# Splitting one product of the first pass's down stage a second time, and putting its queue in source order

## The chip, the cores and the metric

The kernel runs on one core of one Trainium2 chip. The metric is device microseconds (us) of one execution. A core has a matrix engine (PE, whose weight loads are listed as PEld), a vector engine (DVE), an activation engine (ACT), a third elementwise engine (POOL, which also issues the output transfers of this stage) and SyncE (SP), a queue that here does nothing but issue transfers (DMAs). Each engine works through its own list of instructions in order and waits on semaphores for the others.

## What is computed

The reference is a linear attention block and a SwiGLU feed-forward block on the same normalised input, joined by a gate:

```python
B, S, D, F = 1, 2048, 1024, 3584          # all inputs bfloat16, _rng.normal * 0.05
def _B_ref(x, w_gate, w_up, w_down):
    g = _silu(x @ w_gate)
    u = x @ w_up
    return (g * u) @ w_down
x  = A_x
xn = _layernorm(x, axis=-1)
s  = _A_ref(xn, A_wqkv, A_wo)              # linear attention, 32 heads of 32
g  = _silu(_B_ref(xn, B_w_gate, B_w_up, B_w_down))
return x + s * g
```

The change touches only `(g * u) @ w_down`, the silu behind it and `x + s * g`, and these only for one half of the tokens.

## The kernel before

After the attention part the kernel makes two passes over the tokens, 1024 tokens each (`passes = [1, 0]`). A pass has a gate/up stage, which leaves `h = g * u` transposed in one buffer (`hT`), and a down stage. In the first pass the down stage is `emit_down`, in the last pass `emit_down_m`.

Every large product is a Winograd form of Strassen's scheme: a matrix product cut in 2 x 2 blocks is made with seven block products instead of eight, with sums of blocks ahead of and behind them. In `emit_down` the blocks of `h` are A11, A12 (first 512 tokens) and A21, A22 (other 512 tokens), each over 14 chunks of 128 of the contraction (`NFG = 14`), and the output has two halves of 512 columns. So one block product is 4 token blocks `t` of 128, times 14 steps `k`, each a 128x128 by 128x512 matmul. The seven products are 392 such matmuls:

- phase a (`step_a`): the products M1 (into PSUM bank `dx`), M6 (`dy`), M7 and M5 (the two halves of `dzw`). Token blocks are taken in pairs, `hf = 0` (t = 0, 1) and then `hf = 1` (t = 2, 3). The second of a pair runs `LEAD = 6` steps behind the first. `evac_a` makes the sums from PSUM; for `hf = 0` it keeps them in SBUF (`kept`) and frees the banks.
- phase b (`step_b`): M2 = A12 B21 (into `dx`), M4 and M3 (into `dzw`). It takes `hf = 1` first, on top of what phase a left in PSUM, and then `hf = 0` in fresh banks, to which `evac_b` adds what was kept.

The weights come in packs: seven "a" packs of 1 MB (phase a), seven "b" packs of 768 KB (phase b), then the 1 MB packs of the next pass (`pk_g`, `pk_u`: g0, u0, g1, ...). There are eight pack buffers (`NPK`), so a pack can be loaded when an older one is no longer read. `load_w_to(n)` issues the loads of packs up to number n on SP.

The last pass makes four of its seven down products, M2 among them, with the same scheme one level further down: seven sub-products of 256 columns each, over 7 pairs of chunks (`l2_M`, `l2_p`). The weight sums for this are made during the first pass: `l2_early(2, j, False)` makes the four sums of pack j on POOL (L1137), into the unused end of the b pack, and `l2_early(2, j, True)` stores them by three DMAs on SP (L1129 to L1131). In the kernel before they stand in the step loop of phase b, `hf = 1`, one pack every second step, and only the last pass uses them.

The output: `fin` (L1219) multiplies a silu tile by `s`, adds `x` (L1223, L1224, both on DVE), has POOL issue the 128 KB output transfer (L1225) and calls `io_load` for a later tile's `x` and `s` (two 128 KB loads on SP, L1214 and L1215). There are five `io` buffers, so an `io_load` waits until the output transfer of the tile five places back has landed. The order of tiles is the list `fq`. Where `hold[0]` is set, `io_load` only notes the load in `io_due`. `fin` calls put into `deferred` are emitted one by one in the next pass's gate/up loop, each behind one step's evacuation.

The next pass's first operations on DVE are L996, L997 and L1010, which read the PSUM banks of its first group (`yb`, `zw`). `emit_Ssum` (L713 to L716) makes the four input sums for the next pass on DVE. PE runs group g0 (`emit_a`, 16 matmuls), u0 (`emit_a`, 16), then `emit_b` of g0 (12), which adds into g0's `xb` and the two halves of `zw`.

The order on PE, DVE, ACT and POOL is the source order everywhere. On SP it is the source order in the attention part and in the last pass (`manual_schedule`); in the first pass a scheduler places SP's instructions.

Of the kernel before, what the change touches and what calls it, by code (L numbers as in the profile page):

```python
# [21 lines left out]
def kernel(  # L22
# [931 lines left out]
    with ExitStack() as p3:  # L954
# [237 lines left out]
        for p in passes:  # L1192
            if p == passes[-1]:
                fq += [(p, t + dt, cc) for dt, cc in ((0, 0), (TPB, 1), (TPB, 0), (0, 1)) for t in range(TPB)]
                continue
            fq += [(p, t + TPB, 1) for t in range(TPB)]
            for hf in (1, 0):
                for t in (2 * hf, 2 * hf + 1):
                    fq += [(p, t + TPB, 0), (p, t, 1), (p, t, 0)]
# [29 lines left out]
        def emit_down(p, h, base, last, more_S, next_S):  # L1229
# [13 lines left out]

            def alloc(t, phase):
                x_ = pps.tile([P, CW], FP32, name="dx", tag="s")
                y_ = pps.tile([P, CW], FP32, name="dy", tag="s") if phase == "a" else None
                zw = ppd.tile([P, 2, CW], FP32, name="dzw", tag="d")
                bk[t] = (x_, y_, zw)
# [3 lines left out]

            def step_a(t, k):
                if k == 0:
                    alloc(t, "a")
                x_, y_, zw = bk[t]
                S1, S2, S3 = [v[:, k % 2, (t % 2) * P:(t % 2 + 1) * P] for v in s_ring[(t // 2, k // 2)]]
                f, l = k == 0, k == NFG - 1
                mm(x_[:], h[:, 2 * k, t * P:(t + 1) * P], wa(k, 3), f, l)
                mm(y_[:], S2, wa(k, 1), f, l)  # L1260
                mm(zw[:, 0, :], S3, wa(k, 2), f, l)
                mm(zw[:, 1, :], S1, wa(k, 0), f, l)

            def prods_b(t, k, fresh):
                x_, y_, zw = bk[t]
                f, l = fresh and k == 0, k == NFG - 1
                t2 = slice(TB + t * P, TB + (t + 1) * P)
                return [lambda: mm(x_[:], h[:, 2 * k + 1, t * P:(t + 1) * P], wb(k, 0), f, l),
                        lambda: mm(zw[:, 0, :], h[:, 2 * k + 1, t2], wb(k, 2), f, l),
                        lambda: mm(zw[:, 1, :], h[:, 2 * k, t2].bitcast(F16), wb(k, 1), f, l)]  # L1270

            def step_b(t, k, fresh):
                if k == 0 and fresh:
                    alloc(t, "b")
                for f in prods_b(t, k, fresh):
                    f()

            fin_e = (nc.vector, nc.vector, nc.sync if last else nc.gpsimd)
            pend = []

            def evac_a(t, keep):
# [5 lines left out]
                else:  # L1287
                    s1 = k2([P, CW], FP32, "s1")[:]
# [3 lines left out]
                nc.vector.tensor_tensor(out=s2, in0=y_[:], in1=s1, op=ALU.add)  # L1292
                nc.vector.tensor_tensor(out=s3, in0=zw[:, 0, :], in1=s2, op=ALU.add)
                c22 = k2([P, CW], FP32, "c22")[:] if keep else s3
                if keep:
                    nc.vector.tensor_tensor(out=u4, in0=zw[:, 1, :], in1=s2, op=ALU.add)
                nc.vector.tensor_tensor(out=c22, in0=zw[:, 1, :], in1=s3, op=ALU.add)
                g_ = k2([P, CW], BF16, "g22")[:]
                nc.scalar.activation(out=g_, in_=c22, func=ACT.Silu, scale=rch)
                pend.append(lambda: fin(p, t + TPB, 1, g_, *fin_e))  # L1300
                kept[t] = (s1, st[:, 1:3, :]) if keep else s2

            def evac_b(t, fresh):
                x_, _, zw = bk[t]
                d = m4.tile([P, 2, CW], FP32, name="dd", tag="m4")
                g_ = k2([P, 2, CW], BF16, "g12")
                g11 = k2([P, CW], BF16, "g11")[:]
                if fresh:
                    s1, s34 = kept[t]
                    c11 = k2([P, CW], FP32, "c11")[:]  # L1310
                    nc.vector.tensor_tensor(out=d[:], in0=zw[:], in1=s34, op=ALU.add)
                    nc.vector.tensor_tensor(out=c11, in0=x_[:], in1=s1, op=ALU.add)
                    nc.scalar.activation(out=g_[:], in_=d[:], func=ACT.Silu, scale=rch)
                    nc.scalar.activation(out=g11, in_=c11, func=ACT.Silu, scale=rch)
                else:
                    s2 = kept[t]
                    nc.vector.tensor_tensor(out=d[:], in0=zw[:], in1=s2[:, None, :].to_broadcast([P, 2, CW]),
                                            op=ALU.add)
                    nc.scalar.activation(out=g11, in_=x_[:], func=ACT.Silu, scale=rch)
                    nc.scalar.activation(out=g_[:], in_=d[:], func=ACT.Silu, scale=rch)  # L1320
                return [lambda: fin(p, t + TPB, 0, g_[:, 0, :], *fin_e),
                        lambda: fin(p, t, 1, g_[:, 1, :], *fin_e),
                        lambda: fin(p, t, 0, g11, *fin_e)]

            def finish(t):
                ps = [ppd.tile([P, 2, CW], FP32, name="dz", tag="d")[:, 0, :]]
                ps += [pps.tile([P, CW], FP32, name="df%d" % i, tag="s")[:] for i in range(3)]
                s1, s34 = kept[t]
                t1, t2 = slice(t * P, (t + 1) * P), slice(TB + t * P, TB + (t + 1) * P)
                hs_ = [slice(0, 3 * CW // 4), slice(3 * CW // 4, CW)]  # L1330
                for i in range(2):
                    nc.scalar.copy(out=ps[2 + i][:, 0:hs_[i].stop - hs_[i].start], in_=s1[:, hs_[i]])
                for q, (r0, cc) in enumerate(((t + TPB, 0), (t, 1))):
                    for k in range(NFG):
                        lhs = h[:, 2 * k, t2].bitcast(F16) if q else h[:, 2 * k + 1, t2]
                        mm(ps[q], lhs, wb(k, 2 - q), k == 0, k == NFG - 1)
                    d = k2([P, CW], FP32, "d%d" % q)[:]
                    g_ = k2([P, CW], BF16, "g%d" % q)[:]
                    nc.vector.tensor_tensor(out=d, in0=ps[q], in1=s34[:, q, :], op=ALU.add)
                    nc.scalar.activation(out=g_, in_=d, func=ACT.Silu, scale=rch)  # L1340
                    if q == 0:
                        f0 = (r0, cc, g_)
                fin(p, *f0, *fin_e)
                fin(p, r0, cc, g_, *fin_e)
                g11 = k2([P, CW], BF16, "g11")[:]
                for i, cs in enumerate(hs_):
                    o_ = ps[2 + i][:, 0:cs.stop - cs.start]
                    for k in range(NFG):
                        mm(o_, h[:, 2 * k + 1, t1], wb(k, 0)[:, cs], False, k == NFG - 1)
                    nc.scalar.activation(out=g11[:, cs], in_=o_, func=ACT.Silu, scale=rch)  # L1350
                    fin(p, t, 0, g11, *fin_e, cols=cs)

            NS = NFG + LEAD
            for hf in range(2):
                t0, t1 = 2 * hf, 2 * hf + 1
                for st in range(NS):
                    if st == 4:
                        while pend:
                            pend.pop(0)()
# [7 lines left out]
                    if st < NFG:  # L1367
                        step_a(t0, st)
                        if st == NFG - 1:
                            evac_a(t0, hf == 0)  # L1370
                    if st >= LEAD:
                        step_a(t1, st - LEAD)
                        if hf == 1 and (st - LEAD) % 2 == 1:
                            load_w_to(base + NWA + (st - LEAD) // 2 + 2)
                evac_a(t1, hf == 0)
# [3 lines left out]
            if not last:  # L1379
                emit_rcl()  # L1380
                emit_Ssum(passes[passes.index(p) + 1])
            for hf in (1, 0):
                t0, t1 = 2 * hf, 2 * hf + 1
                fresh = hf == 0
                endz = last and fresh
                for st in range(NFG if endz else NS):
                    if st == 4:
                        while pend:
                            pend.pop(0)()
                    if hf == 1 and not last and st % 2 == 1 and 2 in L2:  # L1390
                        if st // 2 < NQ:
                            l2_early(2, st // 2, False)
                        if 0 <= st // 2 - 2 < NQ:
                            l2_early(2, st // 2 - 2, True)
                    if st < NFG:
                        step_b(t0, st, fresh)
                        if st == NFG - 1:
                            fins = evac_b(t0, fresh)
                    if st >= LEAD and not endz:
                        step_b(t1, st - LEAD, fresh)  # L1400
                        if fresh and (st - LEAD) % 2 == 1:
                            load_w_to(base + 2 * NWA + (st - LEAD) // 2 + 2)
                if endz:
                    for f in fins:
                        f()
                    finish(t1)
                    break
                fins2 = evac_b(t1, fresh)
                for f in fins:
# [413 lines left out]
```

## Time and profile before

| | us |
|---|---|
| median of 3 runs (753.15 to 754.32) | 753.2 |
| the profiled execution | 753.18 |
| its span (the profile's clock) | 751.4 |
| first matmul of the first down stage | 413.86 |
| first matmul of phase b | 462.2 |
| first matmul of the second pass | 498.46 |
| first matmul of the last down stage | 667.83 |

All places in time below are microseconds from the start of the span. The 1.8 us between the span and the execution's time lie around the span. The stage that the change touches runs from 413.86 to 498.46, 84.6 us, and its phase b takes 36.2 us. The profile's rows give PE, DVE, ACT and POOL busy times; a matmul's listed duration (379 ns for 512 columns) includes a modelled pipeline end and overlaps the next one's, so the pace of matmuls is read from start to start.

### The profile page before, as it was taken

The page shows a single profiled execution, that of the slowest core. Times are in us where ns is not written, and L with a number is a line of the kernel's source. Part 1 is how long each engine was busy: PE and PEld are TensorE (multiplying, and loading weights), DVE is VectorE, ACT ScalarE, POOL GpSimd, SP SyncE. Part 2 cuts the span into 40 slices and gives each one's busy share as a digit, 9 for nine tenths or more (in the row PEclk, how much of TensorE's full clock was granted, in tenths as well). Part 3 has the DMA queues.
Part 4 walks back from the last instruction along what each step waited for, and adds up shares of the span by engine and source line. Part 5 has one row for each costly group of instructions (what it writes and reads, how often), then busy time and mean ns, then how long its engine had stood idle before and what let it go on. Part 6 is the DMA issues. An engine that isn't in the chain of part 4 may idle for free.

```text
span 751.4 us, 11202 instructions
## 1 busy us (share of the span) xinstructions
PE 744.1 (99%) x3899; PEld 364.9 (49%) x3899; DVE 580.9 (77%) x1054; ACT 383.0 (51%) x549; POOL 395.2 (53%) x492
## 2 busy tenths in 40 slices
PE   8999999999999999999999999999999999999997
PEld 3544544454454444444444444444444444467664
DVE  6687787887697788888889894557777778688857
ACT  5677766889965666756558411132322232332023
POOL 2444799998540265858585021910767576940000
PEclk9999999999999999999999999999999999999999
DMA  9957799869688668888799418789989889478852
GB/s 316 302 145 147 217 335 304 307 146 261 218 203 281 222 225 295 291 310 291 283 304 404 157 42 296 227 261 373 327 302 321 315 285 363 161 224 315 275 187 98
DMA packets 132472, 194.20 MB, mean 258 GB/s; under 512 B 36432, under 2 KB 106192, under 8 KB 122688
## 3 DMA queue, kind: packets, MB, share of 16 engines
q1 hardware_dynamic: 124224, 159.21, 65.7%
q0 software_dynamic: 6752, 31.79, 11.0%
q10 hardware_dynamic: 1440, 2.49, 1.0%
q8 instruction: 30, 0.49, 0.3%
q14 instruction: 26, 0.21, 0.1%
HBM read 122.68 MB, written 63.44 MB: 248 GB/s over the span
## 4 chain that ended last, share of the span: by engine, by line
PE 96%; DVE 2%; ACT 1%; DMA 0%; issue 0%; ACTq 0%; DVEq 0%
PE zw L968 26%; PE kv_ps L556 15%; PE xb L968 13%; PE yb L968 7%; PE q_ps L183 6%; PE dzw L1251 6%; PE dm L1484 6%; PE dm L1448 5%; PE dx L1251 3%; PE fx L818 3%; PE s_ps L776 3%; PE dy L1251 2%; PE kvz L578 1%; PE nd L745 1%; DVE w_sb L311 0%; PE fx L776 0%
## 5 line engine op out<-in xcount | busy, mean ns | idle before, releaser
L968 PEld LDWEIGHTS <-w_sb 128*128 128x128 f16 (+1 forms) x1568 | 152.1, 98 | 182.9 <-DMA w_sb<-pk_u 0.5
L968 PE MATMUL xb<-xnT,w_sb 128*128 128x512 bf16 x448 | 115.0, 379 | 0.0
L556 PE MATMUL kv_ps<-wkv_sb,xnT 128*128 128x512 bf16 x512 | 113.7, 379 | 0.6 <-ACT xnT L545 0.4
L968 PE MATMUL zw<-xnT,w_sb 128*128 128x512 bf16 x448 | 105.8, 379 | 0.0
L968 PE MATMUL zw<-S,w_sb 128*128 128x512 f16 x448 | 105.8, 379 | 0.0
L323 POOL TENSOR_TENSOR w_sb<-w_sb 128x512 f16<-128x512 bf16 x42 | 50.2, 1196 | 95.7 <-DVE w_sb L311 51.3
L288 ACT ACTIVATE w_sb<-w_sb 128x2048 bf16<-128x2048 bf16 x42 | 79.9, 1902 | 4.4 <-DMA w_sb<-in_B_w_up_dram 4.4
L556 PEld LDWEIGHTS <-xnT 128*128 128x128 bf16 x512 | 48.3, 98 | 55.9 <-ACT xnT L545 0.8
L1149 POOL TENSOR_TENSOR w_sb<-w_sb 128x512 f16<-128x512 f16 (+3 forms) x48 | 52.7, 1118 | 29.1 <-DMA w_sb<-wd 28.2
L1044 ACT ACTIVATE sg<-cg 128x1024 bf16<-128x1024 f32 x28 | 29.6, 1057 | 57.4 <-DVE cg L1037 57.4
L183 PE MATMUL q_ps<-xnT,wq_sb 128*128 128x512 bf16 x256 | 58.4, 379 | 0.0
L968 PE MATMUL yb<-S,w_sb 128*128 128x512 f16 x224 | 57.4, 379 | 0.0
L1037 DVE SCALAR_TENSOR_TENSOR cg<-zw,rc_all,s 128x1024 f32<-128x1024 f32 x28 | 35.9, 1284 | 24.5 <-PE zw L968 12.5
L996 DVE SCALAR_TENSOR_TENSOR s<-yb,rc_all,s 128x512 f32<-128x512 f32 x42 | 31.4, 749 | 27.3 <-ACT s L995 27.3
L324 POOL TENSOR_TENSOR w_sb<-w_sb 128x512 f16<-128x512 bf16 x42 | 50.4, 1201 | 3.3
L326 POOL TENSOR_TENSOR w_sb<-w_sb 128x512 f16<-128x512 bf16 x42 | 50.3, 1197 | 0.0
L325 POOL TENSOR_TENSOR w_sb<-w_sb 128x512 f16<-128x512 bf16 x42 | 50.2, 1196 | 0.0
L1225 POOL DMA_DIRECT2D out_dram<-io x16 | 8.7, 544 | 74.5 <-DVE io L1224 74.2
L995 ACT ACTIVATE s<-xb,rcl 128x512 f32<-128x512 f32 x14 | 9.6, 687 | 65.4 <-PE xb L968 65.4
L1251 PE MATMUL dx<-w_sb,hT 128*128 128x512 bf16 x112 | 42.4, 379 | 0.0
L995 ACT ACTIVATE s<-xb,rc_all 128x512 f32<-128x512 f32 x42 | 28.3, 674 | 21.8 <-issue 12.8
L311 DVE TENSOR_SCALAR w_sb<-w_sb,cs_all 128x2048 bf16<-128x2048 bf16 x35 | 36.7, 1048 | 2.8
(221 smaller groups left out, 1334.6 us busy)
## 6 DMA issues: line engine op xcount, KB each, us to landing
w_sb<-pk_g SPq DMA_DIRECT2D x27, 1024.0 KB, 7.3
pk_g<-w_sb SPq DMA_DIRECT2D x14, 1024.0 KB, 5.1
w_sb<-pk_u SPq DMA_DIRECT2D x14, 1024.0 KB, 7.5
pk_u<-w_sb POOLq DMA_DIRECT2D x13, 1024.0 KB, 5.5
w_sb<-l SPq DMA_DIRECT2D x12, 896.0 KB, 4.7
l<-w_sb POOLq DMA_DIRECT2D x9, 896.0 KB, 8.0
w_sb<-in_B_w_gate_dram SPq DMA_DIRECT2D x14, 512.0 KB, 6.5
w_sb<-in_B_w_down_dram SPq DMA_DIRECT2D x28, 256.0 KB, 4.5
```

Source lines behind the costliest of these rows:

```text
L183: nc.tensor.matmul(q_ps[:], lhsT=wq_sb[:, dc, g * P:(g + 1) * P], rhs=xn_ap(dc, btok), start=(dc == 0), stop=(dc == DC - 1))
L288: nc.scalar.activation(out=junk, in_=raw_view(key, t), func=ACT.Square, accum_out=asum[:])
L323: nc.gpsimd.tensor_tensor(out=T1, in0=b12, in1=b11, op=ALU.subtract)
L324: nc.gpsimd.tensor_tensor(out=T2, in0=b22, in1=T1, op=ALU.subtract)
L325: nc.gpsimd.tensor_tensor(out=T3, in0=b22, in1=b12, op=ALU.subtract)
L326: nc.gpsimd.tensor_tensor(out=T4, in0=b21, in1=T2, op=ALU.subtract)
L556: mm = nc.tensor.matmul(kv_ps[:], lhsT=xn_ap(dc, tok), rhs=wkv_sb[:, dc, c * CW:(c + 1) * CW], start=(dc == 0), stop=(dc == DC - 1))
L968: mm = nc.tensor.matmul(out, lhsT=lhs(k), rhs=rhs(k), start=(first and k == 0), stop=(k == HK - 1), skip_group_check=True)
L995: nc.scalar.activation(out=s1[:], in_=x_[:], func=ACT.Copy, scale=rc)
L1149: nc.gpsimd.tensor_tensor(out=b(o_), in0=b(a_), in1=b(b_), op=ALU.subtract)
L1251: nc.tensor.matmul(out, lhsT=lhs, rhs=rhs, start=first, stop=lastk, skip_group_check=True)
L1484: nc.tensor.matmul(out, lhsT=lhs, rhs=w[:, j], start=i == 1 and j == 0, stop=j == NQ - 1, skip_group_check=True)
```

## The change

M2 of the first pass's down stage is now made at the second level, as in the last pass, for all four token blocks at once (`l2_M2`), between the other two products of `hf = 1` and those of `hf = 0`. `step_b` issues only M4 and M3. Of `hf = 0`, four steps of the first block (and two of the second) stand inside `l2_M2` as `fill`; the second block now runs `LB = 2` steps behind, not 6. The weight sums (POOL) stand right behind the issue of the next b pack's load in phase a; four packs' stores stand ahead of phase b, three behind the matmuls of `hf = 1`. The left operand's sums (`lhs12`, `lhs34`) are four new DVE operations of 128x1792. `emit_Ssum` moves behind `l2_M2`. SP is in source order within `emit_down`. The order of output tiles, `fq`, follows. From behind `l2_M2` to behind the last matmul, `io_load` only notes its loads (`hold[0] = -1`); they are issued behind the load of the eighth pack of the next pass. Then `flush(2)` emits two `fin` calls, and the last two are deferred.

```diff
-            for hf in (1, 0):
-                for t in (2 * hf, 2 * hf + 1):
-                    fq += [(p, t + TPB, 0), (p, t, 1), (p, t, 0)]
+            fq += [(p, t + dt, cc) for t in (2, 3) for dt, cc in ((TPB, 0), (0, 1))]
+            fq += [(p, t, 0) for t in (1, 0, 3, 2)]
+            fq += [(p, t + dt, cc) for t in (0, 1) for dt, cc in ((TPB, 0), (0, 1))]
...
+            sp_man = ExitStack()
+            sp_man.enter_context(tc.manual_schedule(engines={mybir.EngineType.SP}))
...
-                return [lambda: mm(x_[:], h[:, 2 * k + 1, t * P:(t + 1) * P], wb(k, 0), f, l),
-                        lambda: mm(zw[:, 0, :], h[:, 2 * k + 1, t2], wb(k, 2), f, l),
-                        lambda: mm(zw[:, 1, :], h[:, 2 * k, t2].bitcast(F16), wb(k, 1), f, l)]
+                mm(zw[:, 0, :], h[:, 2 * k + 1, t2], wb(k, 2), f, l)
+                mm(zw[:, 1, :], h[:, 2 * k, t2].bitcast(F16), wb(k, 1), f, l)
...
+            def lhs12():
+                tt(l2_buf(5, 1), a21, a22)
+                tt(l2_buf(6, 2), sb[5], a11, ALU.subtract)
+            def lhs34():
+                tt(l2_buf(7, 0), a11, a21, ALU.subtract)
+                sb[3] = a21.bitcast(F16)
+                tt(sb[3], a12, sb[6], ALU.subtract)
...
+            def l2_M2(fill):
+                lo, hi = slice(0, CH), slice(CH, CW)
+                bank = [[pps.tile([P, CW], FP32, name="dm", tag="s")[:] for _ in range(2)] for r in range(2)]
+                K = [[kept[2 * r + i][0] for i in range(2)] for r in range(2)]
+                for r in range(2):
+                    l2_p(1, r, bank[r])
+                for r in range(2):
+                    nc.scalar.copy(out=bank[r][1][:, hi], in_=bank[r][0][:, lo])
+                for r in range(2):
+                    l2_p(2, r, bank[r])
+                for r in range(2):
+                    l2_p(5, r, bank[r])
+                    l2_p(6, r, bank[r])
+                    nc.scalar.copy(out=bank[r][1][:, lo], in_=bank[r][1][:, hi])
+                flush()
+                for r in range(2):
+                    l2_p(7, r, bank[r])
+                cs = [m4.tile([P, 2, CW], FP32, name="dc", tag="m4") for r in range(2)]
+                for r in range(2):
+                    (xw, zy), c = bank[r], cs[r]
+                    tt(c[:, 1, hi], zy[:, lo], K[r][1][:, hi])
+                    tt(c[:, 0, hi], zy[:, hi], K[r][0][:, hi])
+                    tt(c[:, 0, lo], xw[:, lo], K[r][0][:, lo])
+                    tt(c[:, 1, hi], xw[:, hi], c[:, 1, hi])
+                fill()
+                for r in range(2):
+                    l2_p(4, r, bank[r])
+                for r in range(2):
+                    (xw, zy), c = bank[r], cs[r]
+                    tt(c[:, 1, lo], zy[:, lo], K[r][1][:, lo])
+                    fins.append((2 * r + 1, 0, silu(c[:, 1], "g11")))
+                    l2_p(3, r, bank[r])
+                    tt(c[:, 0, hi], xw[:, hi], c[:, 0, hi])
+                    fins.append((2 * r, 0, silu(c[:, 0], "g11")))
...
                         if hf == 1 and (st - LEAD) % 2 == 1:
                             load_w_to(base + NWA + (st - LEAD) // 2 + 2)
+                            l2_early(2, (st - LEAD) // 2, False)
...
             load_w_to(base + 2 * NWA + 1)
-            if not last:
-                emit_rcl()
-                emit_Ssum(passes[passes.index(p) + 1])
...
+            lhs34()
+            emit_rcl()
+            for j in range(NQ - 3):
+                l2_early(2, j, True)
+            for st in range(NS):
+                if st < NFG:
+                    step_b(TPB - 2, st, False)
+                    if st == NFG - 1:
+                        flush()
+                        evac_b(TPB - 2)
+                if st >= LEAD:
+                    step_b(TPB - 1, st - LEAD, False)
+            for j in range(NQ - 3, NQ):
+                l2_early(2, j, True)
+            evac_b(TPB - 1)
+            LB, FB = 2, 4
+            def b0(st):
+                if st < NFG:
+                    step_b(0, st, True)
+                if st >= LB:
+                    step_b(1, st - LB, True)
+                if st == NFG - 1:
+                    flush()
+                    evac_b(0)
+            def fill():
+                for st in range(FB):
+                    b0(st)
+            l2_M2(fill)
+            emit_Ssum(passes[passes.index(p) + 1])
+            hold[0] = -1
+            for st in range(FB, NFG + LB):
+                load_w_to(base + 2 * NWA + (st - LB) // 2 + 1)
+                b0(st)
+            load_w_to(base + 3 * NWA + 1)
+            evac_b(1)
+            hold[0] = False
+            while io_due:
+                io_due.popleft()
+                io_load()
+            flush(2)
+            while fins:
+                deferred.append(lambda f=fins.popleft(): fin(p, *f, nc.vector, nc.vector, nc.gpsimd))
+            sp_man.close()
```

`flush(n)` emits up to n of the pending `fin` calls (all without a number). `l2_p(i, r, bank)` issues seven matmuls of 256 columns: sub-product i for the token blocks of pair r.

More of the change, by code (lines that the diff above doesn't have):

```diff
@@ L1227, in fin, with emit_down @@
                 io_load()
-        def emit_down(p, h, base, last, more_S, next_S):
+        def emit_down(p, h, base, more_S, next_S):
             def wa(k, q):
@@ L1242, in emit_down, with tt @@
             kept = {}
[L1244 to L1248, printed above, removed]
+            sp_man = ExitStack()
+            sp_man.enter_context(tc.manual_schedule(engines={mybir.EngineType.SP}))
             def mm(out, lhs, rhs, first, lastk):
                 nc.tensor.matmul(out, lhsT=lhs, rhs=rhs, start=first, stop=lastk, skip_group_check=True)
+            def tt(out, a, b_, op=ALU.add):
+                nc.vector.tensor_tensor(out=out, in0=a, in1=b_, op=op)
             def step_a(t, k):
                 if k == 0:
-                    alloc(t, "a")
+                    bk[t] = [pps.tile([P, CW], FP32, name=nm, tag="s") for nm in ("dx", "dy")]
+                    bk[t].append(ppd.tile([P, 2, CW], FP32, name="dzw", tag="d"))
                 x_, y_, zw = bk[t]
@@ L1262, in step_a, with step_b, flush, silu @@
                 mm(zw[:, 1, :], S1, wa(k, 0), f, l)
-            def prods_b(t, k, fresh):
-                x_, y_, zw = bk[t]
+            def step_b(t, k, fresh):
+                if k == 0 and fresh:
+                    bk[t] = [ppd.tile([P, 2, CW], FP32, name="dzw", tag="d")]
+                zw = bk[t][-1]
                 f, l = fresh and k == 0, k == NFG - 1
                 t2 = slice(TB + t * P, TB + (t + 1) * P)
-                return [lambda: mm(x_[:], h[:, 2 * k + 1, t * P:(t + 1) * P], wb(k, 0), f, l),
-                        lambda: mm(zw[:, 0, :], h[:, 2 * k + 1, t2], wb(k, 2), f, l),
-                        lambda: mm(zw[:, 1, :], h[:, 2 * k, t2].bitcast(F16), wb(k, 1), f, l)]
[L1272 to L1279, printed above, removed]
+                mm(zw[:, 0, :], h[:, 2 * k + 1, t2], wb(k, 2), f, l)
+                mm(zw[:, 1, :], h[:, 2 * k, t2].bitcast(F16), wb(k, 1), f, l)
+            fins = deque()
+            def flush(n=99):
+                while fins and n:
+                    fin(p, *fins.popleft(), nc.vector, nc.vector, nc.gpsimd)
+                    n -= 1
+            def silu(c, nm):
+                g_ = k2([P, CW], BF16, nm)[:]
+                nc.scalar.activation(out=g_, in_=c, func=ACT.Silu, scale=rch)
+                return g_
             def evac_a(t, keep):
@@ L1287, in evac_a @@
                 else:
-                    s1 = k2([P, CW], FP32, "s1")[:]
+                    s1 = x_spare[t - TPB // 2][:, 3, :]
                     s3 = k2([P, CW], FP32, "s3")[:]
@@ L1291, in evac_a @@
                 nc.scalar.copy(out=s1, in_=x_[:])
-                nc.vector.tensor_tensor(out=s2, in0=y_[:], in1=s1, op=ALU.add)
-                nc.vector.tensor_tensor(out=s3, in0=zw[:, 0, :], in1=s2, op=ALU.add)
+                tt(s2, y_[:], s1)
+                tt(s3, zw[:, 0, :], s2)
                 c22 = k2([P, CW], FP32, "c22")[:] if keep else s3
                 if keep:
-                    nc.vector.tensor_tensor(out=u4, in0=zw[:, 1, :], in1=s2, op=ALU.add)
-                nc.vector.tensor_tensor(out=c22, in0=zw[:, 1, :], in1=s3, op=ALU.add)
@@ L1298, in evac_a @@
[L1298 to L1304, printed above, removed]
+                    tt(u4, zw[:, 1, :], s2)
+                tt(c22, zw[:, 1, :], s3)
+                fins.append((t + TPB, 1, silu(c22, "g22")))
+                kept[t] = (s1, st[:, 1:3, :] if keep else s2[:, None, :].to_broadcast([P, 2, CW]))
@@ L1305, in evac_b @@
+            def evac_b(t):
                 d = m4.tile([P, 2, CW], FP32, name="dd", tag="m4")
                 g_ = k2([P, 2, CW], BF16, "g12")
[L1307 to L1351, printed above, removed]
@@ new lines, in evac_b, with l2_buf @@
+                tt(d[:], bk[t][-1][:], kept[t][1])
+                nc.scalar.activation(out=g_[:], in_=d[:], func=ACT.Silu, scale=rch)
+                fins.extend([(t + TPB, 0, g_[:, 0, :]), (t, 1, g_[:, 1, :])])
+            A = quads(h, 1, 0)
+            aq = [A[:, k].rearrange("p j (r t n) -> p j r t n", r=2, t=2) for k in range(2)]
+            a11, a12, a21, a22 = aq[0][:, :, :, 0], aq[1][:, :, :, 0], aq[0][:, :, :, 1], aq[1][:, :, :, 1]
+            sb = {}
+            def l2_buf(i, s):
+                t = sp.tile([P, HK, TB], F16, name="S%d" % s, tag="S%d" % s)
+                sb[i] = t[:].rearrange("p a b -> p (a b)")[:, 0:2 * NQ * P].rearrange("p (j r n) -> p j r n", j=NQ, r=2)
+                return sb[i]
@@ new lines, in lhs12, with l2_p @@
+            def lhs12():
[5 more added lines that the diff above has]
+                tt(sb[3], a12, sb[6], ALU.subtract)
+            def l2_p(i, r, bank):
+                half, y0 = {1: (0, 0), 2: (0, 0), 5: (0, 1), 3: (0, 1), 6: (1, 1), 7: (1, 0), 4: (1, 0)}[i]
+                out = bank[half][:, y0 * CH:(y0 + 1) * CH]
+                lhs = {1: a11, 2: a12, 4: a22}.get(i)
+                lhs = sb[i] if lhs is None else lhs
+                for j in range(NQ):
+                    w = w_tiles[(p, "b", j)][:].rearrange("p h a b -> p (h a b)")
+                    if i <= 3:
+                        k, c = {1: (0, 0), 2: (1, 0), 3: (1, 1)}[i]
+                        w = w[:, 0:6 * CW].rearrange("p (k q c n) -> p q k c n", k=2, q=3, c=2)[:, M_PACK[2][1], k, c]
+                    else:
+                        w = w[:, 6 * CW:8 * CW].rearrange("p (b n) -> p b n", b=4)[:, (5, 6, 7, 4).index(i)].bitcast(F16)
+                    mm(out, lhs[:, j, r], w, i == 1 and j == 0, j == NQ - 1)
@@ L1357, in emit_down @@
                     if st == 4:
-                        while pend:
-                            pend.pop(0)()
+                        flush()
                     if hf == 0:
@@ L1370, in emit_down @@
                             evac_a(t0, hf == 0)
+                            if hf == 1:
+                                lhs12()
                     if st >= LEAD:
@@ L1378, in emit_down @@
             load_w_to(base + 2 * NWA + 1)
-            if not last:
-                emit_rcl()
-                emit_Ssum(passes[passes.index(p) + 1])
[L1382 to L1409, printed above, removed]
-                    f()
-                if fresh:
-                    deferred.extend(fins2)
-                else:
-                    for f in fins2:
-                        f()
@@ new lines, in emit_down @@
+            evac_b(TPB - 1)
[6 more added lines that the diff above has]
+                if st == NFG - 1:
+                    flush()
+                    evac_b(0)
[5 more added lines that the diff above has]
+            hold[0] = -1
@@ L1788 @@
             else:
-                emit_down(p, h, base, last_pass, more_S, next_S)
+                emit_down(p, h, base, more_S, next_S)
             base += 2 * NWA
```

## The prediction

> **What bounds the kernel now.** I read the busy times and the chain of waits first, then the stretches around the stage.
>
> ```profile
> PE 744.1 (99%) x3899; PEld 364.9 (49%) x3899; DVE 580.9 (77%) x1054; ACT 383.0 (51%) x549; POOL 395.2 (53%) x492
> ...
> PE 96%; DVE 2%; ACT 1%; DMA 0%; issue 0%; ACTq 0%; DVEq 0%
> ```
>
> PE is the bound. In the table of stretches (busy us of PE, PEld, DVE, ACT, POOL, then granted clock, DMA share, GB/s) it has no gap in phase b, nor in the start of the second pass, where the DMA engines are almost full:
>
> ```profile
> 462.20:480.00 17.80, 17.80 (x84) 8.13 (x83) 9.63 (x13) 2.70 (x4) 8.96 (x15) 1.00 0.98 346
> 480.00:498.40 18.40, 18.40 (x87) 8.29 (x86) 9.63 (x15) 3.60 (x4) 8.90 (x14) 1.00 0.62 193
> 498.40:520.00 21.60, 21.60 (x102) 9.59 (x100) 18.55 (x28) 7.88 (x11) 2.70 (x5) 1.00 0.95 365
> ```
>
> So work taken off PE is gained whole, and a wait of PE is lost whole. The timeline of PE gives its paces (start, us, line, count):
>
> ```profile
> 1.49 4.07 PE L592 MATMUL warm_ps<-warm 128*128 128x512 bf16 x11 [1.49 <-DVE warm L589]
> ...
> 413.86 0.38 PE L1251 MATMUL dx<-w_sb,hT 128*128 128x512 bf16 x1
> ...
> 498.46 1.03 PE L968 MATMUL yb<-S,w_sb 128*128 128x512 f16 x4
> ...
> 502.06 1.04 PE L968 MATMUL yb<-S,w_sb 128*128 128x512 f16 x4
> ...
> 670.89 4.75 PE L1484 MATMUL dm<-w_sb 128*128 128x256 f16 x42
> 675.47 4.75 PE L1484 MATMUL dm<-w_sb,hT 128*128 128x256 bf16 x42
> ```
>
> A matmul of 512 columns takes (498.46 - 413.86)/392 = 0.2158 us, one of 256 columns in the second-level form (680.06 - 670.89)/84 = 0.1092 (680.06 is where the next row starts).
>
> **The change, part by part.** *M2 on PE.* 56 x 0.2158 = 12.09 us go, 7 x 2 x 7 = 98 matmuls x 0.1092 = 10.70 come: -1.38. The other 112 matmuls stay. New times: phase b starts at 462.20; M4 and M3 of the second half end at 462.20 + 56 x 0.2158 = 474.29; 70 sub-product matmuls to 481.93, 12 of `fill` to 484.52, 28 more to 487.58; the last 44 end at T = 497.08, where the second pass can begin.
>
> *What lies under PE.* The four left sums are 128x1792, beside `emit_Ssum`'s 128x2048 at 1.22 us: some 1.1 us each. Two fall in DVE's idle 3.83 us ahead of 462.37, two take the place in which `emit_Ssum` stood (464.58 to 469.4). PSUM copies (0.36 us, L1496 and L1504) have the 28 matmuls of the next sub-product in front of them; in the last pass they cost PE 0.3 us once. POOL's sums follow the packs: b1 is issued when SP gets past the `io` loads, 450.76 as before, and lands 5.6 us later; six packs at 2.67 to 2.79 us each, from this row and the one before it (456.48, 2.67):
>
> ```profile
> 471.91 13.97 POOL L1137 TENSOR_TENSOR w_sb<-w_sb 128x256 f16<-128x256 bf16 x20
> ```
>
> end near 473; PE wants the last at 478. I cost all this at nothing. Behind POOL's sums stand, in its queue, the two output transfers that release the `io` buffer of the eighth tile: issued at 473.1, landed 5.6 later, the load 2.7 more: 482.0. DVE's first sums of M2 stand behind that tile's `fin` (0.9 us) and PE's sub-product 4 behind them at 484.5. Slack about 1 us; each us beyond it would cost PE one.
>
> *The wait that it adds.* The built program's order settles where the fourteenth tile stands. Its `x` and `s` are the first loads that `hold` puts off: on SP they come behind u0, g1, u1, g2, u2, g3, u3, and u3's buffer is free only at T. Its `fin`, the second of `flush(2)`, stands on DVE ahead of L996, L997 and L1010 of the second pass's first group, with nothing of that group before it. What a small load behind packs costs, the issue times on SP and the landings show (the landing lines are the answers for a stretch around one issue each: 500.7 to 500.9, 504.0 to 504.2, 508.9 to 509.1; the last number is us to landing):
>
> ```profile
> 500.79 0.38 SPq L265 DMA_DIRECT2D w_sb<-pk_g  x1
> ...
> 504.07 0.39 SPq L265 DMA_DIRECT2D w_sb<-pk_u  x1
> ...
> 508.94 0.33 SPq L1214 DMA_DIRECT2D io<-in_A_x_dram  x1
> ```
>
> ```profile
> w_sb<-pk_g SPq DMA_DIRECT2D x1, 1024.0 KB, 6.8
> ...
> w_sb<-pk_u SPq DMA_DIRECT2D x1, 1024.0 KB, 17.4
> ...
> io<-in_A_x_dram SPq DMA_DIRECT2D x1, 128.0 KB, 12.9
> ```
>
> Six packs land from 507.6 to 521.5, one per 2.78 us, and the 128 KB load lands at 521.8, right behind the last, although quiet ones took 2.4 to 2.9. The queue is served in order. Before, no `fin` needed such a load soon: SP was held up, the `io` loads came at 488.69 to 500.3, ahead of the packs.
>
> [...] Here the landings keep the order; by a free order the first rival below would be the result.
>
> After the change u0 is issued at 489.0: its buffer is free at 487.6, but the thirteenth tile's load stands ahead on SP and waits for the eighth tile's output (`fin` 482.9, landed 5 us behind its issue, 488.5). Later packs are issued faster than one per 2.78 us, so the queue stays full: u0 lands 6.8 us later, 495.8; u3 at 495.8 + 6 x 2.78 = 512.5; the tile's two loads at 0.37 each (521.84 - 521.47 above): 513.2. On DVE follow the `fin`, 0.88, and two evacuations:
>
> ```profile
> 502.79 0.74 DVE L996 SCALAR_TENSOR_TENSOR s<-yb,rc_all,s 128x512 f32<-128x512 f32 x1
> 503.63 0.75 DVE L997 SCALAR_TENSOR_TENSOR s<-zw,rc_all,s 128x512 f32<-128x512 f32 x1
> ```
>
> 1.59 us from the start of L996 to the end of L997: 515.7. PE needs that bank when `emit_b` of g0 reaches `zw`, after 36 matmuls: 497.08 + 7.77 = 504.85. Wait: 10.8 us. Bounds: 430 GB/s (the stretches' upper values), thus 2.45 us a pack, and u0 at 487.6 give 7.3; 3.0 us a pack and u0 at 490 give 13.
>
> *The restart.* No row shows PE after a long wait inside the kernel. The nearest is the first row above: eleven matmuls after idleness took 4.07 us, where 11 x 0.2158 + 0.16 = 2.53 is the later pace, 1.5 more (the granted clock reads 1.00 there too). From the other side, at full pace PE would wait about 1.0 us for L1037 to free g0's `zw` bank: at 518.9 DVE is still on u0's evacuations. These overlap, so +1.0 to +1.7; I take 1.5, the row.
>
> [...]
>
> *The pack that was late.* Before, PE reached u0 at 498.46 + 16 x 0.2158 = 501.92 and started at 502.06. Now u0 lands at 495.8 and is wanted at 500.5: -0.14.
>
> Sum: -1.38 - 0.14 + 10.8 + 1.5 = +10.8. On the profiled execution's 753.18, which equals the median to 0.02, that is 764.0. Own range of this case: -1.5 + 7.3 + 1.0 = +6.8 to -1.5 + 13 + 1.7 = +13.2, so 760 to 766.4.
>
> **Rivals.** *The tile's load comes in time (not slower).* The place is SP's load of the fourteenth tile; it decides from a landing near 502. If it is not held behind the packs, it is issued when the ninth tile's output has landed: `emit_Ssum` ends on DVE near 493, `fin` 0.9, output 5.1 to 8.1 (shown in this stretch), 499.5 to 502.5; 2.5 to land, then 0.9 and 1.6 to the end of L997: 504.5 to 507.5 against 504.85. PE waits 0 to 2.7 us and the time is 751.7 to 754.4. For it: quiet loads take 2.5 us. Against it: the 12.9. Chance 0.14.
>
> *PE waits inside M2 as well.* If POOL's sums end 2 to 4 us later (b3 to b6 land as late as before, 464 to 470), the eighth tile's `fin` keeps DVE from M2's sums and PE stops ahead of sub-product 4 for 1 to 3 us. u0's issue moves with T then, so the later wait stays: 765 to 767. For it: a slack of 1 us over four steps. Against it: b3 to b6 are no longer held up by SP's stores. Chance 0.12.
>
> *A shorter wait.* Packs land at 2.2 us or less, or the load lands ahead of the last packs: PE waits 2 to 7 us, 755 to 760. Chance 0.06; the stretches show no such rate for long.
>
> **How the numbers follow.** The forecast has 0.68, the rivals 0.14, 0.12 and 0.06. The time is the forecast's, 764.0. The range, 756 to 768, takes in the two slower rivals and leaves out the first. Below 0.2% (1.5 us, about what can be told from no change) lies part of the first rival: faster 0.07, within 0.2% 0.06, slower 0.87.
>
> **What would show it.** In the profile after: 98 matmuls of 256 columns in this stage at 0.109, phase b about 34.9 us long; SP issuing `io` loads behind seven packs near 498 to 501; a DVE wait on `io<-s_dram` of 10 to 14 us ahead of L1223, the last before L996; PE idle 8 to 13 us on L997 ahead of the `zw` matmuls of L968; the next matmuls slow. The forecast is wrong if that `io` load lands before 505, or if DVE does L996 before it.

## The result, and the profile after

The changed kernel takes 764.2 us (median of 4 runs, 764.1 to 765.4), the kernel before 753.2 (4 runs, 752.6 to 754.3): a ratio of 1.0148, 95% interval 1.0131 to 1.0166. The profiled execution took 764.32, its span 762.4, 11.0 more than before.

The busy times and the chain of waits of the kernel after, from its page:

```profile
PE 745.2 (98%) x3941; PEld 369.9 (49%) x3941; DVE 587.1 (77%) x1068; ACT 384.0 (50%) x553; POOL 396.9 (52%) x492
...
PE 92%; issue 3%; DMA 2%; DVE 2%; ACT 1%; POOL 0%; SPq 0%; DVEq 0%; ACTq 0%; POOLq 0%
```

PE's share of the chain fell from 96% to 92%: something else now sets the end for a while. (PE's listed busy time is 1.1 us higher, although the second-level M2 takes PE less time: 83.38 against 84.60 in the down stage, but 170.84 against 169.37 in the second pass, where the matmuls behind that wait run slowly, as shown below, and 411.54 against 410.73 ahead of the two.) Where, the timeline of PE after shows (start, us, line, count; in brackets the idle time before the row and its releaser):

```profile
414.00 0.38 PE L1247 MATMUL dx<-w_sb,hT 128*128 128x512 bf16 x1
...
474.44 1.69 PE L1247 MATMUL dm<-w_sb,hT 128*128 128x256 bf16 x14
477.37 1.69 PE L1247 MATMUL dm<-w_sb,hT 128*128 128x256 bf16 x14 [1.24 <-ACT dm L1352]
...
498.62 1.03 PE L968 MATMUL yb<-S,w_sb 128*128 128x512 f16 x4
...
515.97 3.35 PE L968 MATMUL zw<-xnT,w_sb 128*128 128x512 bf16 x8 [9.41 <-DVE s L1010]
519.15 1.03 PE L968 MATMUL yb<-S,w_sb 128*128 128x512 f16 x4
...
678.87 3.22 PE L1522 MATMUL dm<-w_sb,hT 128*128 128x256 bf16 x28
```

Three readings follow. The down stage, from its first matmul to that of the second pass, is as long as before: 498.62 - 414.00 = 84.62 against 84.60; a wait of 1.24 us inside M2 stands against what M2 saves. The second pass, from there to the first matmul of the last down stage, takes 678.87 - 498.62 = 180.25 against 667.83 - 498.46 = 169.37, so +10.88, and this is the whole loss. In it PE stands still for 9.41 us ahead of the first `emit_b`, and the eight matmuls behind the wait take 519.15 - 515.97 = 3.18 us, where 8 x 0.2158 = 1.73 is the pace elsewhere.

What DVE did meanwhile, its timeline after:

```profile
500.52 0.43 DVE L1224 TENSOR_TENSOR io<-g,io 128x512 bf16<-128x512 bf16 x1
512.73 0.43 DVE L1223 TENSOR_TENSOR g<-g,io 128x512 bf16<-128x512 bf16 x1 [11.78 <-DMA io<-s_dram]
513.19 0.42 DVE L1224 TENSOR_TENSOR io<-g,io 128x512 bf16<-128x512 bf16 x1
513.53 0.74 DVE L996 SCALAR_TENSOR_TENSOR s<-yb,rc_all,s 128x512 f32<-128x512 f32 x1
514.38 0.75 DVE L997 SCALAR_TENSOR_TENSOR s<-zw,rc_all,s 128x512 f32<-128x512 f32 x1
515.16 0.75 DVE L1010 SCALAR_TENSOR_TENSOR s<-zw,rc_all,s 128x512 f32<-128x512 f32 x1
```

The fourteenth tile's `fin` waits 11.78 us for its `s` and holds L996, L997 and L1010 behind it, although their data were there by about 502 (run 1 below, whose second pass begins 0.44 us earlier, has L996 at 501.40). L1010's end, 515.91, releases PE.

The issues on SP after, and the landings (answers for the stretches 498.8 to 499.0 and 502.3 to 502.5; the last number is us to landing):

```profile
488.66 0.35 SPq L265 DMA_DIRECT2D w_sb<-pk_u  x1
...
498.82 0.32 SPq L265 DMA_DIRECT2D w_sb<-pk_u  x1
501.93 0.33 SPq L1214 DMA_DIRECT2D io<-in_A_x_dram  x1
502.31 0.48 SPq L1215 DMA_DIRECT2D io<-s_dram  x1
```

```profile
w_sb<-pk_u SPq DMA_DIRECT2D x1, 1024.0 KB, 13.1
...
io<-s_dram SPq DMA_DIRECT2D x1, 128.0 KB, 10.4
```

Seven packs are issued from 488.66 (u0) to 498.82 (u3). The last lands at 511.9, the tile's `s` right behind it at 502.31 + 10.4 = 512.7.

### The profile page after: what moved, and what is told of

Its sections match the earlier page's. It is cut to its first block, busy times and chain, and to the rows that moved or that the text cites. A ratio compares the mean times of both kernels' runs of the same rounds, so it can differ in the third digit from the quotient of the medians.

```text
span 762.4 us, 11305 instructions
## 1 busy us (share of the span) xinstructions
PE 745.2 (98%) x3941; PEld 369.9 (49%) x3941; DVE 587.1 (77%) x1068; ACT 384.0 (50%) x553; POOL 396.9 (52%) x492
## 4 chain that ended last, share of the span: by engine, by line
PE 92%; issue 3%; DMA 2%; DVE 2%; ACT 1%; POOL 0%; SPq 0%; DVEq 0%; ACTq 0%; POOLq 0%
PE zw L968 25%; PE kv_ps L556 15%; PE xb L968 12%; PE q_ps L183 6%; PE yb L968 6%; PE dm L1522 5%; PE dzw L1247 5%; PE dm L1486 5%; PE fx L818 3%; PE s_ps L776 2%; PE dx L1247 2%; PE dy L1247 2%; DMA io<-s_dram 1%; PE kvz L578 1%; PE nd L745 1%
## 5 line engine op out<-in xcount | busy, mean ns | idle before, releaser
L996 DVE SCALAR_TENSOR_TENSOR s<-yb,rc_all,s 128x512 f32<-128x512 f32 x42 | 31.4, 748 | 28.5 <-ACT s L995 28.5
L183 PEld LDWEIGHTS <-wq_sb 128*128 128x128 bf16 x256 | 24.4, 98 | 27.5
## 6 DMA issues: line engine op xcount, KB each, us to landing
w_sb<-in_B_w_gate_dram SPq DMA_DIRECT2D x14, 512.0 KB, 6.7
```

The source lines that it names most:

```text
L183: nc.tensor.matmul(q_ps[:], lhsT=wq_sb[:, dc, g * P:(g + 1) * P], rhs=xn_ap(dc, btok), start=(dc == 0), stop=(dc == DC - 1))
```

## The experiments

Each expectation stood before its run. Times are medians; the kernel before took 753.5 (13 runs) beside the first four and 753.4 (21 runs) beside the last three.

**1. The late tile's `fin` out of the way.** The loads stay behind the packs; only DVE's order changes.

```diff
-            flush(2)
+            flush(1)
+            deferred.append(lambda: None)
```

> The changed kernel, with the fourteenth tile's `fin` moved from ahead of the second pass's first evacuation into the deferred list, one step later than the first deferred place; the loads stay where they are, behind seven packs. Theory (the load lands late because SP's queue is served in order, and DVE's in-order `fin` passes the wait on to PE): DVE reaches L996 near 501, PE waits for it less than 1 us, the clock is not lowered; 9.4 us of wait and 1.45 us of slow restart go: 764.2 - 10.9 = 753.3, within 0.5. Rival (PE waits for something else, for instance DVE's longer list or the packs themselves): 763 to 764.

Measured: 753.26 us, ratio to before 0.9995 (0.9985 to 1.0004). DVE's timeline:

```profile
501.40 0.75 DVE L996 SCALAR_TENSOR_TENSOR s<-yb,rc_all,s 128x512 f32<-128x512 f32 x1 [0.89 <-ACT s L995]
```

L996 runs at 501.40 and PE has no wait in the second pass; that pass takes 667.39 - 498.18 = 169.21 us. So the place of this one `fin` on DVE was worth the whole loss, and this length is the base for the next ones.

**2. The loads not held back.** They now stand on SP behind u2, ahead of g3 and u3.

```diff
             emit_Ssum(passes[passes.index(p) + 1])
-            hold[0] = -1
```

> The changed kernel without holding back the loads: the four pairs of `io` loads stand on SP behind u2, ahead of g3 and u3. Theory: the fourteenth tile's load is issued when the ninth tile's output has landed, near 502, and lands right behind u2, near 507.5 and not 512.7; L1010 ends near 510.8, PE waits some 4.3 us and not 9.4; the restart may or may not be slow: 757.5 to 759.3. Rival (the load is late because the DMA engines are full, wherever it stands): within 1 us of 764.2.

Measured: 759.62 us, ratio 1.0082 (1.0067 to 1.0097). Timeline of PE:

```profile
499.37 1.03 PE L968 MATMUL yb<-S,w_sb 128*128 128x512 f16 x4
...
511.82 3.57 PE L968 MATMUL zw<-xnT,w_sb 128*128 128x512 bf16 x8 [4.52 <-DVE s L1010]
515.19 1.91 PE L968 MATMUL yb<-S,w_sb 128*128 128x512 f16 x4
```

The load was issued at 502 and the `fin` ran at 508.6, not 512.7: with two packs fewer ahead of it the landing comes 4 us sooner, and the wait is 4.5 as expected. The time is 0.3 above the range. Even this wait was followed by a slow restart: the second pass took 675.82 - 499.37 = 176.45, that is 169.21 + 4.52 + 2.72. The traced execution was the longest of the four (761.16), so its restart may be longer than the median's.

**3. The late loads on another queue.** Only the fourteenth tile's two loads are issued by ACT.

```diff
+            first_due = True
             while io_due:
                 io_due.popleft()
-                io_load()
+                io_load(eng=nc.scalar if first_due else None)
+                first_due = False
```

> The changed kernel, with the fourteenth tile's two loads issued by ACT and not by SP, at the same place of the program; packs and all other loads as they were. Theory (order within SP's queue is what holds the load): it is issued near 502, when the ninth tile's output has landed, and lands within 3 to 6 us, 505 to 508, far ahead of u3; PE waits 1 to 4.5 us: 754 to 759. Rival (the 16 DMA engines are full until 512 and any load waits as long): it lands near 512, 764.

Measured: 763.73 us, ratio 1.0133 (1.0118 to 1.0148): the rival held. ACT's timeline, and the landing over the stretch 485 to 520:

```profile
502.08 0.51 ACTq L1216 DMA_DIRECT2D io<-s_dram  x1
```

```profile
io<-in_A_x_dram ACTq DMA_DIRECT2D x1, 128.0 KB, 7.4
io<-s_dram ACTq DMA_DIRECT2D x1, 128.0 KB, 9.8
```

Issued at 502.08 on a queue with nothing else in it, the load still landed at 511.9. The packs came later in this trace than in the changed kernel's: u3, issued at 498.93, took 14.9 us and landed at 513.8. So the load passed u3 by 1.9 us, where in SP's queue it came 0.8 behind it. By these two traces the order within SP's queue is worth some 2.7 us of the delay. The rest remained on an empty queue: four packs were still in flight, and the 16 engines moved 417 GB/s on average from 498 to 512. The pair landed at 509.1 and 511.9, between u2 (508.3) and u3. Why two 128 KB loads did not get through sooner stays open.

**4. M2's copies ahead of the silu.** In M2, sub-product 1 goes to half a PSUM bank, ACT copies that half aside (L1352), and sub-product 2 adds into it. The copies stood behind the silu of the fourth token block on ACT.

```diff
                 for r in range(2):
                     nc.scalar.copy(out=bank[r][1][:, hi], in_=bank[r][0][:, lo])
+                evac_b(TPB - 1)
...
-            evac_b(TPB - 1)
```

> The changed kernel, with the evacuation of the fourth token block behind the first two PSUM copies of M2 on ACT, so that its silu no longer stands ahead of them. Theory: the 1.24 us wait of PE on L1352 falls to 0.3 or less; sub-product matmuls, u0's buffer and so the late load all come about 1 us earlier, the 9.4 us wait stays: 764.2 - 1.0 = 763.2, within 0.4. Rival (PE has slack there, since it waits later anyway for a load whose time is set by the packs alone, with u0 not moving): 764.2.

Measured: 764.95 us, ratio 1.0154 (1.0137 to 1.0171); no gain. Timeline of PE:

```profile
413.70 0.38 PE L1247 MATMUL dx<-w_sb,hT 128*128 128x512 bf16 x1
...
496.92 1.03 PE L968 MATMUL yb<-S,w_sb 128*128 128x512 f16 x4
...
515.79 3.57 PE L968 MATMUL zw<-xnT,w_sb 128*128 128x512 bf16 x8 [10.93 <-DVE s L1010]
```

The wait inside M2 is gone and the stage takes 83.22 us, 1.38 less than before: exactly M2's price as predicted. The other half of the expectation failed: the load did not come 1 us earlier. SP, which issued stores and `io` loads without a break from 483.94 at the latest, reached u0 at 489.02, so the load landed when it had (`fin` at 512.55) and PE waited 10.93 instead of 9.41. The time is 0.7 above the changed kernel's; the restart was longer as well (last section). A gain ahead of a wait for something that does not move is lost in the wait.

**5. Both edits, 1 and 4.**

> The changed kernel with both edits: the fourteenth tile's `fin` deferred by two steps, and the fourth block's evacuation behind M2's first copies. Theory: without the late wait, what the copies give (1.24 to 1.4 us of stage length, 83.2 against 84.6) reaches the end: the first one alone took 753.26, so 752.0, 0.2% below the kernel before (ratio 0.998). Rival (the second pass takes the gain back, its DVE or packs being the bound there): 753.3, ratio 1.000.

Measured: 751.82 us, ratio 0.998 (0.9971 to 0.9989). The stage takes 497.23 - 414.01 = 83.22, the second pass 666.45 - 497.23 = 169.22. This version is below both kernels, and 1.6 us below the kernel before: 1.4 is what M2 at the second level saves, and nearly all of the rest is the pack that was late (169.22 against 169.37).

**6. The kernel before, with SP in source order in this stage.** No other edit.

```diff
+            sp_man = ExitStack()
+            sp_man.enter_context(tc.manual_schedule(engines={mybir.EngineType.SP}))
...
+            sp_man.close()
```

> The kernel before, with nothing changed but SP in source order within the first pass's down stage. Theory (what stands ahead on SP decides when packs land): two more pairs of `io` loads come ahead of u0, the last waits for an output that lands near 499.8, u0 is issued near 500.7 and not 495.05 and lands near 507.5; PE wants it at 501.9 and waits 5.6 us, and restarts slowly, 1.5 to 2.5: 753.5 + 7 to 8, 760.5 to 761.6. Rival (source order costs nothing by itself, the packs being needed later): 753.5.

Measured: 754.58 us, ratio 1.0016 (1.0007 to 1.0026): the direction of the theory, a sixth of its size. Issue on SP, and PE's row:

```profile
498.35 0.38 SPq L265 DMA_DIRECT2D w_sb<-pk_u  x1
```

```profile
503.84 1.04 PE L968 MATMUL yb<-S,w_sb 128*128 128x512 f16 x4 [1.20 <-DMA w_sb<-pk_u]
```

u0 is issued 3.3 us later than before and PE waits for it, but 498.35 is 2.35 earlier than I had worked out from the old run's output landing, and the pack landed 5.4 us behind its issue, not 6.8. A wait of 1.2 us left no slow restart: the four matmuls behind it took 504.71 - 503.84 = 0.87 us, and 4 x 0.2158 = 0.86 is the pace elsewhere.

**7. The changed kernel without SP's source order.**

```diff
-            sp_man = ExitStack()
-            sp_man.enter_context(tc.manual_schedule(engines={mybir.EngineType.SP}))
...
-            sp_man.close()
```

> The changed kernel without SP's source order in the down stage: the scheduler places SP's instructions again. Seven packs still stand ahead of the fourteenth tile's loads, only the stores of M2's weight sums move ahead. Theory: the late load and both waits stay: 763.5 to 765. Rival (the source order is what costs): below 757.

Measured: 768.13 us, ratio 1.0198 (1.0184 to 1.0212), slower than the theory's range too. Waits of PE in this kernel (us in total, times, longest):

```profile
PE zw L968 <- DVE s L1010: 10.3, 1, 10.3
...
PE dzw L1244 <- DMA w_sb<-wd: 1.4, 1, 1.4
```

The late load stays, as expected. What I had missed: the scheduler puts the stores of pack b0 and b1 ahead of b3's load, and the last four b packs are issued from 459.5 to 462.8 as in the kernel before; with M2 gone from the step loop of phase b, PE runs through the packs faster, and waits for one. In the trace the down stage takes 86.49 us (84.62 in the changed kernel) and the second pass 182.02 (180.25). The source order is what this change needs, not what it suffers from.

## Why the prediction was right, step by step

**The bound and the price of M2: right.** -1.38 us is what runs 4 and 5 show (84.60 to 83.22).

**What lies under PE: one item wrong.** I costed the PSUM copies at nothing, "the 28 matmuls of the next sub-product in front of them". For the first copies that is false: the next sub-product, 2, has only 14 matmuls, and it adds into the half that they read, so it must wait for them, and on ACT they stood behind a silu:

```profile
475.90 1.15 ACT L1309 ACTIVATE g<-dd,hsc 128x1024 bf16<-128x1024 f32 x1 [1.88 <-DVE dd L1250]
476.95 0.63 ACT L1352 COPY dm<-dm 128x256 f32<-128x256 f32 x2
```

Two copies end at 477.6 at the latest; the first releases PE at 477.37, 1.24 us late (ACT after; run 4 confirms it). The rest cost nothing, as predicted, though two sizes were off. DVE's four sums took 1.3 to 1.5 us each, not 1.1. POOL's sums ended at 472.7 (predicted near 473), but the outputs behind them landed 3.1 us after their issue and not 5.6, so the eighth tile's `fin` ran at 478.4 with 0.2 of wait and not at 482.0. The slack there was some 4 us, and the rival that put a wait there did not come.

**The added wait: right in place, its cause right in part, with sizes off that nearly cancel.** u0 was issued at 488.66 (489.0), and the load landed at 512.7 (513.2). The first hit was luck: the issue did not wait for the eighth tile's output, which had landed at 483.3 (issued at 479.60, 3.7 us to landing); SP was busy with stores and `io` loads without a break from 475.87 to 488.5. u0 landed sooner than predicted, 5.1 us behind its issue and not 6.8, and the packs then came every (511.9 - 493.8)/6 = 3.0 us and not 2.78. PE's wait was 9.41 us against 10.8: the second pass began at 498.62 and not 497.08, because of the copies and a start 0.14 later (-1.54); the load came 0.5 sooner; but PE needed L1010's end, not L997's (+0.78), since the wait on DVE is for the last reader of both halves. That the pace of the packs and u0's own landing cancel is luck as well. That the missed copies did not show in the time is not: what they added to the stage they took from a wait whose end did not move, as run 4 shows from the other side. Run 1 shows that this `fin` was the cause; runs 2 and 4 that the landing moves with the packs ahead and not with PE.

The explanation of the late landing was too narrow: I put it to SP's queue being served in order. By run 3 that order is worth some 2.7 us, and a load in another queue was late too. The rival that the load comes in time fell, and its price was wrong as well: it gave a load that is not held behind the packs 2.5 us to land, and run 3's took 9.8.

**The restart: right.** Predicted 1.5; the second pass less 169.21 less the wait gives 180.25 - 169.21 - 9.41 = 1.63. In the traces of runs 2, 3, 4 and 7 the same term is 2.4 to 2.7 (last section), above my upper 1.7, so that the size fits here is in part luck, the more as the prediction's row ran at a granted clock of 1.00 (the kernel before, stretches from 0 to 6 us). No run shows that 1.7 as a limit; the five traces with a long wait show 1.6 to 2.7 in its place. The granted clock of the stretches after (the third number from the end) shows it:

```profile
507.00:509.00 2.00, 0.00 (x0) 0.00 (x0) 0.00 (x0) 0.00 (x0) 0.00 (x0) 0.93 1.03 434
509.00:511.00 2.00, 0.00 (x0) 0.00 (x0) 0.00 (x0) 0.00 (x0) 0.00 (x0) 0.50 0.96 385
...
518.00:519.00 1.00, 1.00 (x4) 0.39 (x3) 0.58 (x1) 0.00 (x0) 0.00 (x0) 0.52 0.07 23
519.00:520.00 1.00, 1.00 (x6) 0.43 (x5) 0.64 (x1) 0.00 (x0) 0.00 (x0) 1.00 0.00 0
```

The clock falls to half some 2.2 us after PE's last matmul (506.5 to about 508.7) and comes back about 3 us after PE resumes.

**The late pack: right.** u0's first matmul is at 502.08, 3.46 behind the pass's first, with no wait: -0.14.

## What to carry to other kernels

When loads are held back behind a burst of large ones, look for the first instruction that needs one of them and for what stands behind it on its in-order engine: one elementwise operation in front of a PSUM evacuation cost 11 us here, and moving it by two steps cost nothing. Before saving work ahead of a wait, ask what ends that wait: while the load did not move, M2's 1.4 us could not be seen, and only both edits together gave them. The first copies out of PSUM, whose source is accumulated into next, were on the matrix engine's path here (a wait of 1.24 us), whatever lay between them and their own reader.

## What the runs showed of the hardware

A wait of PE of 4.5 us was enough for a slow restart in run 2, and it was not cheaper than that of a long one: taken as above, 1.6 us behind 9.4 us of wait (the changed kernel), 2.4 behind 8.5 (run 3: 678.90 - 498.73 = 180.17), 2.55 behind 10.9 (run 4: 679.61 - 496.92 = 182.69), 2.5 behind 10.3 (run 7), 2.7 behind 4.5 (run 2). Each is one traced execution; from run 2's median, 759.62 - 753.26 - 4.52 leaves 1.8. In run 2 the clock fell about 2.9 us after the last matmul and stayed at one half to 517, 5 us after PE resumed:

```profile
510.00:511.00 1.00, 0.00 (x0) 0.00 (x0) 0.88 (x2) 0.00 (x0) 0.30 (x1) 0.60 1.03 403
...
516.00:517.00 1.00, 1.00 (x4) 0.40 (x3) 1.00 (x2) 0.25 (x1) 0.00 (x0) 0.50 0.39 128
```

The return came 2.9 us after PE resumed in the changed kernel, some 5 in run 2 and 4.8 in run 4 (PE resumed at 515.79; the granted clock reads 0.50 until 520 and 0.68 from 520 to 521). The fall came 2.1 to 2.9 us after the last matmul in these three (run 4: it ended at 504.86, and the granted clock reads 1.00 until 507 and 0.50 from there). For run 7 the fall is an estimate: a mean granted clock of 0.993 over a span of 766.1 us makes 10.0 to 11.5 us at one half, and the four matmuls from 522.16 took 1.54 us, which puts the return near 523.5; so the fall was near 512.0 to 513.5, 3.5 to 5.1 us after the last matmul (ended at 508.47). By that estimate a wait of 4.5 us need not always reach the fall. The wait of 1.2 us in run 6 did not: the mean granted clock of that execution is 1.0. Why the moments of the fall and of the return differ from run to run is not shown.

And a 128 KB load on a queue of its own took 9.8 us with four 1 MB packs still in flight on another (run 3), where 2.4 to 2.9 us was usual in quiet stretches (the kernel before, loads issued from 476.2 to 477.6 and from 492.2 to 500.3).
